# Clustered attention and token mixing on one core: slot lists for the two row halves of the scores, PSUM banks by a plan, and six weight splits moved behind attention

## The chip, the cores and the metric

One core of a Trainium2 chip runs the whole program. The metric is the device time of one execution in microseconds, the median of the runs shown. One profiled execution of the kernel before gives the trace that all durations below come from.

## The reference, cut to what matters

```
# q, k, v: (4, 8, 768, 64), centroids: (8, 16, 64)
q_assign = argmax(normalised q . normalised centroids); k_assign likewise
mask = q_assign[:, :, :, None] == k_assign[:, :, None, :]
scores = where(mask, q k^T / sqrt(64), -1e9)
attn = exp(scores - rowmax); attn /= sum(attn) + 1e-9
x = attn @ v, heads side by side: (4, 768, 512)

theta = x @ w_theta
zr, zi = x * cos(theta), x * sin(theta)
y = w_tok_r @ zr + w_tok_i @ zi          # over the 768 tokens
u = x + y
out = u + maximum(u @ w_ch, 0)
```

The four weights arrive as 64-bit floats, the rest as 32-bit floats.

## The kernel before, in words

**Two stages.** Attention runs first, over 16 pairs of heads (`NPAIR`); each pair has 12 units (`NU`): 2 halves of the query axis (`a`, 384 columns each) times 6 blocks of 128 keys (`i`). So there are 192 units (`NUT`), numbered `u`. The mixing stage follows: for each of the 4 batches 6 token blocks, each with its angle (`theta`, into `tp`) and its share of the token mixing (`mix`, into `y`), then the channel product (`channel`).

**A unit.** The two heads of a pair lie in partitions 0 to 63 (`j` = 0) and 64 to 127 (`j` = 1) of the tiles `hq`, `lq`, `hk`, `lk` (high and low parts of q and k), `mq` and `mk` (one-hot cluster codes, and in row 32 of each half the shift of the row maximum). A score tile `sc` of one unit and one half is four products of 64 rows by 384 columns on PE, and products of the two halves run side by side in PE's two row halves. ACT takes the exponential out of PSUM into `at` (line 437), POOL adds three units of `at` into `acc`, and two units later PE multiplies `at` with v (`av`, line 509). The row maxima come ten units ahead (`LEAD`): a tile `m` is two times two products, and DVE reduces it (line 396).

**A round.** The loop takes two units a round. PE's row halves are filled in twelve steps, here called slots: four with both halves of unit u, four with half 0 of unit u+1 beside the maximum of half 1, then `av` of units u-2 and u-1 and the round's side products, then four with half 1 of u+1 beside the maximum of half 0. Side products are `lg` (cluster logits of a pair three ahead), `lt` and `rt`/`mt` (transposes), and `sm` (row sums). The order on each engine is the order in which the code is written: `in_order` chains the instructions of PE, DVE, ACT, POOL and SP in attention. Tables say at which unit a side job is written (`A_UNITS`, `W_UNITS`, `SUMS`, `NORM`, `ADDS`).

**PSUM.** Of the eight banks the two `m` tiles take four, `av` one, and three banks (`ps`) go round in order for `sc`, `lg`, `rt`, `mt` and `sm`.

**Weights.** A weight is turned from 64 to 32 bits and split in a high and a low part: an absolute value on ACT, four operations on DVE (lines 137 to 146), a copy on ACT (`hi`) and a subtraction on POOL (`lo`). In attention sixteen such chunks are written, one per pair; the last six (the token weights of blocks 3 to 5) are only converted, stored to DRAM (`wd`), loaded again at the start of the mixing stage (`kept`, `late`), and split there with the subtraction on DVE (line 791). `w_ch` is converted there too, through four buffers (`u_tile`). In the mixing stage the scheduler orders the instructions.

Of the kernel before, what the change touches and what calls it, by code (L numbers as in the profile page):

```python
# [19 lines left out]
N_M = 2  # L20
# [21 lines left out]
def kernel(  # L42
# [62 lines left out]
    ncl = cpool.tile([P, 1], F32, name="ncl")  # L105
    nc.vector.tensor_scalar_mul(ncl, mcl, -1.0)
# [43 lines left out]
    def split_w(hi, lo, src, cols, new, eng, most, kept=None):  # L150

        def chunk(sl):
            w = yield from to_f32(src[:, sl], sl.stop - sl.start, new)
            yield
            if kept is not None:
                nc.sync.dma_start(out=kept[:, sl], in_=w)
                return
            nc.scalar.copy(out=hi[:, sl], in_=w)
            eng.tensor_tensor(out=lo[:, sl], in0=w, in1=hi[:, sl].bitcast(F32), op=ALU.subtract)
# [15 lines left out]
    w_d = {(t, x): dram.tile([P, S], F32, name=f"wd{t}{x}") for t in range(EARLY, NT) for x in "ri"}  # L175
# [6 lines left out]
    ps = actx.enter_context(tc.tile_pool(name="ps", bufs=8 - 2 * N_M - N_AV, space=PSUM))  # L182
# [16 lines left out]
    def bank(name):  # L199
        return ps.tile([P, 512], F32, tag="bank", name=name)  # L200
# [47 lines left out]
    def assign(pi):  # L248
# [23 lines left out]
        for t in range(HS // P):  # L272
# [57 lines left out]
        mq = st[pi]["mq"]  # L330
        if pi == 1:

            nc.gpsimd.tensor_scalar(out=mq, in0=cl["q"], scalar1=mcl, scalar2=None, op0=ALU.is_equal)
        else:
# [86 lines left out]
    def score_products(u, j, banks=None):  # L421
# [5 lines left out]
        sc = banks[:, j] if banks else ps.tile([P, 512], F32, tag="bank", name=f"sc{u}_{j}")  # L427
# [88 lines left out]
    def weighted_out(u):  # L516
        pi, a, i = split_u(u)
        s = st[pi]
        if i == NT - 1:

# [14 lines left out]
    def early_weights():  # L535
# [5 lines left out]
        for t in range(EARLY, NT):  # L541
            for x, src in (("r", wrT), ("i", wiT)):
                yield from split_w(
                    None, None, src[t * P:(t + 1) * P], S, raw_pair, nc.gpsimd, CKE, kept=w_d[t, x])
# [107 lines left out]
    A_UNITS = (-9, -4, -2, -1, 2, 2, 3, 6, 7, 7.9)  # L652
# [8 lines left out]
    A_THIRD = (-9, -1, 0, 1, 4, 4, 5, 7, 8, 9)  # L661
    W_EVERY = 12
# [39 lines left out]
    while u <= NUT or todo:  # L702
# [8 lines left out]
        if 0 <= u < NUT:  # L711
            both(score_products, u, exps)
            add_exps(u)
            if ahead < NUT:
                scores_beside_max(u + 1, ahead, 0)
# [6 lines left out]
        if 0 < u <= NUT:  # L722
            weighted(u - 2)
            weighted(u - 1)
            if ahead >= NUT:
                weighted_out(u - 1)
        pieces(u)
        if 0 <= u < NUT:
            if ahead < NUT:
                scores_beside_max(u + 1, ahead, 1)  # L730
            else:

                both(score_products, u + 1, exps, *([m_tile(f"sc{u + 1}")] if u < NUT - 6 else []))
            add_exps(u + 1)
        if 0 < u and ahead < NUT:
            weighted_out(u - 1)
# [270 lines left out]
```

## Time and profile before

| | |
|---|---|
| median of 3 runs (lowest to highest) | 792.06 us (789.42 to 792.98) |
| the profiled execution, its span | 792.87 us, 791.1 us |
| granted TensorE clock over the span | 0.991 |
| PE, DVE, ACT, POOL busy | 774.3, 572.6, 386.5, 488.3 us |
| attention's last exponentials end | about 449.5 us into the span |
| the first token mixing product | 462.23 us into the span |

Busy time of PE is that of matmuls that overlap, so PE reads as busy even where its instructions start later than they could: in attention the starts of successive matmuls have to be read. "Idle before" names the engine whose signal came last. Times inside the span are microseconds from its start.

### The profile page before, as it was taken

The numbers are of one execution on the slowest core, as the hardware profiler recorded it, in microseconds if no ns is written. First come the engines' busy times: TensorE is split into PE (matmuls) and PEld (weight loads), VectorE is DVE, ScalarE is ACT, GpSimd is POOL, SyncE is SP. The second block draws the span as 40 slices with busy tenths as digits, with TensorE's granted clock in tenths as the row PEclk, the third lists the DMA queues.
The fourth block names the chain that finished last, engine by engine and source line by source line (L and its number), as shares of the span: only waits on it lengthen the run. The fifth ranks groups of instructions, "written<-read, shape, count | busy, mean of one in ns | idle before, by whom it ended". The sixth has DMA issues, their size and how long they took to land.

```text
span 791.1 us, 14306 instructions
## 1 busy us (share of the span) xinstructions
PE 774.3 (98%) x5538; PEld 572.9 (72%) x5538; DVE 572.6 (72%) x688; ACT 386.5 (49%) x777; POOL 488.3 (62%) x284
## 2 busy tenths in 40 slices
PE   6999999999999999999999799999999999999998
PEld 4656665666656565656665488899889988899998
DVE  5789999999999999999989659954445433634322
ACT  3366666767676676767556436341334123403310
POOL 3388789999999999888988432561215122332131
PEclk9899999999999999999999999999999999999999
DMA  3132324332433244324343467115011411030001
GB/s 120 61 98 72 93 95 151 93 123 91 151 104 125 81 149 151 119 84 164 112 161 109 101 182 206 24 31 173 15 27 28 160 27 27 14 94 15 1 21 61
DMA packets 81583, 73.43 MB, mean 93 GB/s; under 512 B 59588, under 2 KB 65324, under 8 KB 81132
## 3 DMA queue, kind: packets, MB, share of 16 engines
q1 hardware_dynamic: 81228, 72.10, 30.5%
q8 instruction: 43, 0.70, 0.4%
q10 hardware_dynamic: 288, 0.43, 0.1%
q14 instruction: 24, 0.20, 0.1%
HBM read 57.08 MB, written 15.32 MB: 92 GB/s over the span
## 4 chain that ended last, share of the span: by engine, by line
PE 91%; DVE 5%; DMA 2%; issue 1%; SPq 1%; ACT 1%; DVEq 0%
PE y L876 26%; PE sc L374 24%; PE av L509 15%; PE tp L608 8%; PE cy L899 5%; PE m L374 4%; PE cp L899 3%; PE sm L476 2%; PE lg L263 2%; PE y L899 1%; DVE acc L452 1%; PE lt L275 1%; DVE nm L396 1%; PE mt L404 1%; DVE xl L583 1%
## 5 line engine op out<-in xcount | busy, mean ns | idle before, releaser
L437 ACT ACTIVATE at<-sc 128x384 f32<-128x384 f32 x384 | 173.6, 493 | 96.0 <-PE m L374 50.5
L396 DVE TENSOR_REDUCE nm<-m 128x1 f32<-128x768 f32 x192 | 179.6, 945 | 21.4 <-PE m L374 18.3
L448 POOL TENSOR_TENSOR acc<-at,at 128x768 f32<-128x768 f32 x64 | 129.9, 2030 | 36.0 <-ACT at L437 36.0
L374 PE MATMUL m<-hk,hq 64*128 64x384 f32 x384 | 147.1, 387 | 0.9 <-DVE nm L396 0.8
L509 PE MATMUL av<-at,vt 128*64 128x384 f32 x768 | 145.7, 499 | 1.4 <-ACT at L437 1.2
L830 POOL TENSOR_TENSOR zlc<-ab,zhc 128x512 fp32r<-128x512 f32 x24 | 32.1, 1336 | 173.2 <-ACT zhc L828 173.2
L448 POOL TENSOR_TENSOR acc<-acc,at 128x768 f32<-128x768 f32 x64 | 132.4, 2068 | 10.1 <-ACT at L437 8.0
L374 PE MATMUL m<-mk,mq 64*128 64x384 f32 x384 | 127.7, 336 | 0.8 <-DVE mk L303 0.8
L374 PE MATMUL sc<-hq,hk 64*128 64x384 f32 x384 | 116.6, 388 | 0.5 <-ACT at L437 0.5
L374 PEld LDWEIGHTS sc<-hq,hk 64*128 64x128 f32 x384 | 55.8, 184 | 62.7 <-issue 27.9
L374 PE MATMUL sc<-mq,mk 64*128 64x384 f32 x384 | 97.6, 335 | 0.0
L374 PE MATMUL sc<-hq,lk 64*128 64x384 f32 x384 | 97.3, 334 | 0.0
L374 PE MATMUL sc<-lq,hk 64*128 64x384 f32 x384 | 97.3, 334 | 0.0
L509 PEld LDWEIGHTS av<-at,vt 128*64 128x64 f32 x768 | 46.7, 136 | 60.5 <-issue 53.6
L374 PEld LDWEIGHTS m<-hk,hq 64*128 64x128 f32 x384 | 70.7, 185 | 3.4 <-DVE nm L396 2.8
L374 PEld LDWEIGHTS m<-mk,mq 64*128 64x128 f32 x384 | 71.6, 188 | 1.1 <-ACT hq L356 1.1
L613 DVE TENSOR_SCALAR kk<-tp 128x512 int32<-128x512 f32 x24 | 16.4, 683 | 77.2 <-PE tp L608 77.2
L452 DVE TENSOR_TENSOR acc<-acc,acc 128x768 f32<-128x768 f32 x30 | 70.6, 2354 | 0.0
L581 ACT CAST xh<-xT 128x512 fp32r<-128x512 f32 x23 | 14.3, 622 | 99.7 <-PE tp L608 99.7
L890 POOL TENSOR_TENSOR ul<-xT,uh 128x384 fp32r<-128x384 f32 (+1 forms) x36 | 33.5, 957 | 35.4 <-ACT uh L889 34.9
L374 PEld LDWEIGHTS sc<-lq,hk 64*128 64x128 f32 x384 | 54.9, 186 | 0.0
L374 PEld LDWEIGHTS sc<-mq,mk 64*128 64x128 f32 x384 | 54.7, 184 | 0.0
(160 smaller groups left out, 1710.3 us busy)
## 6 DMA issues: line engine op xcount, KB each, us to landing
rawq<-in_qT_dram SPq DMA_DIRECT2D x16, 384.0 KB
vt<-in_v_dram SPq DMA_DIRECT2D x16, 384.0 KB
rb<-sd SPq DMA_DIRECT2D x32, 192.0 KB
xT_d<-xt SPq DMA_DIRECT2D x16, 384.0 KB
xb<-xT_d SPq DMA_DIRECT2D x96, 64.0 KB
rawk<-in_kT_dram SPq DMA_DIRECT2D x15, 384.0 KB
w<-in_wrT_dram SPq DMA_DIRECT2D x6, 768.0 KB
w<-in_wiT_dram SPq DMA_DIRECT2D x6, 768.0 KB
```

The source lines that it names most:

```text
L374: nc.tensor.matmul(out, lhsT=stat[r, cols], rhs=mov[r, over], start=start, stop=stop)
L396: nc.vector.tensor_reduce(out=s["nm", a][:, j, i // 2:i // 2 + 1], in_=s["m", j][:, :, 0:HS], op=ALU.max, axis=AX.XY, negate=True)
L437: last_exp[0] = nc.scalar.activation(out=s["at", a, i][:, j], in_=s["sc", j], func=AF.Exp, scale=SCALE)
L448: last_acc[0] = nc.gpsimd.tensor_tensor(out=s["acc", a, x], in0=prev, in1=at, op=ALU.add)
L452: nc.vector.tensor_tensor(out=s["acc", a, 0], in0=s["acc", a, 0], in1=s["acc", a, 1], op=ALU.add)
L509: nc.tensor.matmul(s["av"][64 * j:64 * j + 64], lhsT=s["vt"][:, i, j, :], rhs=s["at", a, i][:, j], start=(i == 0), stop=(i == NT - 1))
L608: nc.tensor.matmul(tp, lhsT=xx[:, c, :], rhs=w_th[c][k], start=(n == 0), stop=(n == 3 * NCT - 1))
L613: nc.vector.tensor_scalar_mul(kk, tp, INV_2PI)
L830: nc.gpsimd.tensor_tensor(out=zl, in0=tr, in1=zh.bitcast(F32), op=ALU.subtract)
L876: nc.tensor.matmul(y_at(b, d, c0, c1), lhsT=zz[:, d * P:(d + 1) * P], rhs=ww[:, c0:c1], start=first and lead, stop=last, skip_group_check= ...
L890: nc.gpsimd.tensor_tensor(out=ul[:, d, :], in0=x, in1=uh[:, d, :].bitcast(F32), op=ALU.subtract)
L899: nc.tensor.matmul(cp, lhsT=w_c[d][k][:, e * P:(e + 1) * P], rhs=uu[:, d, :], start=(n == 0), stop=(n == 3 * NCT - 1), skip_group_check=True)
```

## The change

Five things change.

1. **Slot lists.** `two_units` writes the twelve slots of a round with a list for each half. Half 0: the last product left over from the round before (slot 0), a maximum (slots 1 to 4), scores of unit u (5 to 8), scores of unit u+1 (9 to 11, the fourth product carried into the next round's slot 0). Half 1: scores of u (0 to 3), a maximum (4 to 7), scores of u+1 (8 to 11). All of `av` and the side products follow slot 11.
2. **Banks by a plan.** The three banks get a buffer each, and `bank` gives out the one that by a count of slots comes free first: a score tile counts as free five slots after its last product, a side tile eight slots after the round's products.
3. **Assignment codes.** `mk` is made by one ACT operation and `mq` by one DVE operation; before, `mq` took two on ACT and `mk` one on DVE. The comparison `eq` stays in PSUM, and its product with the codes reads PSUM.
4. **Weights.** The six chunks of blocks 3 to 5 are no longer converted in attention. `late` loads them as 64-bit floats through the four `u_tile` buffers, in halves of 384 columns (twelve pieces), converts them and splits them with the subtraction on POOL. The ten that stay are spread at two in three pairs.
5. **Copies of `av`** (`weighted_out`) are written in the next round, behind slot 3.

The diff, cut:

```diff
-    w_d = {(t, x): dram.tile([P, S], F32, name=f"wd{t}{x}") for t in range(EARLY, NT) for x in "ri"}
...
-    ps = actx.enter_context(tc.tile_pool(name="ps", bufs=8 - 2 * N_M - N_AV, space=PSUM))
+    NB = 8 - 2 * N_M - N_AV
+    ps = actx.enter_context(tc.tile_pool(name="ps", bufs=1, space=PSUM))
...
-    def bank(name):
-        return ps.tile([P, 512], F32, tag="bank", name=name)
+    clock = [0.0]
+    free_at = [0.0] * NB
+    SLOTS, AV_SLOTS, EXP_SLOTS = 12, 8, 5
+
+    def bank(name, until=None):
+        x = min(range(NB), key=lambda i: (free_at[i], i))
+        free_at[x] = until if until is not None else clock[0] + AV_SLOTS
+        return ps.tile([P, 512], F32, tag=f"bank{x}", name=name)
...
-            out=eq, in0=ltv, in1=mx.unsqueeze(2).broadcast_to([P, NG, C]), op=ALU.is_equal)
-        yield
-
-        nc.vector.tensor_tensor(out=eq, in0=eq, in1=wb, op=ALU.mult)
+            out=ltv, in0=ltv, in1=mx.unsqueeze(2).broadcast_to([P, NG, C]), op=ALU.is_equal)
+        nc.vector.tensor_tensor(out=eq, in0=ltv, in1=wb, op=ALU.mult)
+        yield
...
-            nc.scalar.activation(out=mq, in_=cl["q"], func=AF.Abs, bias=ncl)
-            yield
-            nc.scalar.activation(out=mq, in_=mq, func=AF.Relu, scale=-1.0, bias=1.0)
+        nc.scalar.activation(out=st[pi]["mk"], in_=cl["k"], func=AF.Abs, scale=kscale, bias=kbias)
         yield
         nc.vector.tensor_scalar(
-            out=st[pi]["mk"], in0=cl["k"], scalar1=mcl, scalar2=mbi, op0=ALU.not_equal, op1=ALU.mult)
+            out=st[pi]["mq"], in0=cl["q"], scalar1=mcl, scalar2=-1.0, op0=ALU.is_equal, op1=ALU.mult)
...
-    def scores_beside_max(u, v, j):
-
-        interleave(score_products(u, j), max_products(v, 1 - j))
-        exps(u, j)
-        max_of(v, 1 - j)
+    carry = []
...
+    def two_units(u, v):
+        rows = {(0, 0): carry[0]} if carry else {}
+        first = [(exps, u - 1, 0), (add_exps, u - 1)] if carry else []
+        carry.clear()
+        t0 = clock[0]
+
+        def scores(u, j, start, until):
+            for slot, x in enumerate(score_products(u, j, until=t0 + until + EXP_SLOTS), start):
+                if slot < SLOTS:
+                    rows[j, slot] = x
+                else:
+                    carry.append(x)
...
+        begin = {
+            0: (scores, u, 1, 0, 4), 1: (maxima, 0, 1), 4: (maxima, 1, 4), 5: (scores, u, 0, 5, 9),
+            8: (scores, u + 1, 1, 8, 12), 9: (scores, u + 1, 0, 9, SLOTS + AV_SLOTS + 1)}
+        end = {
+            0: first, 3: [(exps, u, 1), (weighted_out, u - 3)], 4: [(max_of, v, 0)], 7: [(max_of, v, 1)],
+            8: [(exps, u, 0), (add_exps, u)], 11: [(exps, u + 1, 1)]}
...
-    A_UNITS = (-9, -4, -2, -1, 2, 2, 3, 6, 7, 7.9)
+    A_UNITS = (-9, -4, -2.5, -1, 2, 2, 3, 7, 7.9)
...
-        stages(W_FIRST if x == 0 else [W_EVERY * (x - 1) + k for k in W_UNITS], gen)
+        stages(W_FIRST if x == 0 else [NU * (3 * (x - 1) // 2) + k for k in W_UNITS], gen)
...
-            for w, x in ((w_r, "r"), (w_i, "i")):
-                hi, lo = w[t]
-                kept = u_tile("kept").rearrange("p c s -> p (c s)").bitcast(F32)[:, 0:S]
-                nc.sync.dma_start(out=kept, in_=w_d[t, x])
-                nc.scalar.copy(out=hi, in_=kept)
-                nc.vector.tensor_tensor(out=lo, in0=kept, in1=f(hi), op=ALU.subtract)
+            for w, src in ((w_r, wrT), (w_i, wiT)):
+                for gen in split_w(*w[t], src[t * P:(t + 1) * P], S, wt_pair, nc.gpsimd, CK):
+                    run(gen)
```

**PE, round of unit 92, where `mt` and `lg` are written.** Names read: `sc93_0` is unit 93, half 0; `m102_1` a maximum; `av`, `mt` and `lg` as above. Before:

```order
L374 MATMUL sc93_0_3153<-mq_1_147,mk_1_148 128x384
L374 MATMUL m102_1_3155<-mk_2_157,mq_2_156 128x384
L509 MATMUL av90_3168<-at90_3084,vt7_2781 64x384 x2
L509 MATMUL av90_3168<-at91_3097,vt7_2781 64x384 x2
L404 MATMUL mt80_3177<-identf_64,nm96_2977 6x128
L263 MATMUL lg10_3183<-rawq10_3024,cb_194 32x384
L263 MATMUL lg10_3183<-rawk10_3026,cb_194 32x384
...
L374 MATMUL sc93_1_3193<-hq_1_143,hk_1_145 128x384
L374 MATMUL m102_0_3194<-hk_2_154,hq_2_152 128x384
L374 MATMUL sc93_1_3193<-lq_1_144,hk_1_145 128x384
```

With the change:

```order
L378 MATMUL sc93_0_3142<-hq_1_145,lk_1_148 128x384
L378 MATMUL sc93_1_3137<-mq_1_149,mk_1_150 128x384
L552 MATMUL av90_3152<-at90_3056,vt7_2753 64x384 x2
L552 MATMUL av90_3152<-at91_3082,vt7_2753 64x384 x2
L408 MATMUL mt80_3161<-identf_64,nm96_2938 6x128
L273 MATMUL lg10_3167<-rawq10_2997,cb_196 32x384
L273 MATMUL lg10_3167<-rawk10_2999,cb_196 32x384
...
L378 MATMUL sc93_0_3142<-mq_1_149,mk_1_150 128x384
L378 MATMUL sc94_1_3180<-hq_1_145,hk_1_147 128x384
L378 MATMUL m104_0_3184<-hk_2_156,hq_2_154 128x384
L378 MATMUL sc94_1_3180<-lq_1_146,hk_1_147 128x384
```

The fourth product of `sc93_0` now stands behind `av`, `mt` and `lg`. In this round `mt` and `lg` take the two banks that the plan has free, so `sc94_1`, the next row, is given the bank of `sc93_0` itself. That is so in 13 rounds (u = 8, 20, ... 152). In 32 other rounds, after a single side tile, the score tile that begins in slot 5 has the bank of the tile that ended in slot 0; in the plain rounds the closest reuse is slot 3 to slot 9.

**ACT at the same place.** `mr` and `lgs` copy `mt` and `lg` out of PSUM; `wi` is a weight's high part. Before:

```order
L437 ACTIVATE at93_3152<-sc93_0_3153 128x384
L158 CAST wi1_hi_115<-w32_2837 128x768
L415 CAST mr80_3179<-mt80_3177 6x128
L267 COPY lgs10_3188<-lg10_3183 128x384
L437 ACTIVATE at93_3152<-sc93_1_3193 128x384
```

With the change:

```order
L441 ACTIVATE at93_3136<-sc93_1_3137 128x384
L161 CAST wi0_hi_121<-w32_2822 128x768
L419 CAST mr80_3163<-mt80_3161 6x128
L277 COPY lgs10_3172<-lg10_3167 128x384
L441 ACTIVATE at93_3136<-sc93_0_3142 128x384
L441 ACTIVATE at94_3179<-sc94_1_3180 128x384
```

The exponential of `sc93_0` has moved behind the two copies.

**POOL, first batch of the mixing stage.** `zlc` and `zls` are the low parts of the rotated block (batch, block), `wr4_lo` that of a token weight. Before:

```order
L830 TENSOR_TENSOR zlc0_3_6242<-ab0_3_6231,zhc0_3_6241 128x512
L830 TENSOR_TENSOR zls0_3_6248<-r0_3_6212,zhs0_3_6247 128x512
L159 TENSOR_TENSOR wch0_lo_6039<-wtmp_6358,wch0_hi_6038 128x512
L830 TENSOR_TENSOR zlc0_4_6341<-ab0_4_6330,zhc0_4_6340 128x512
L830 TENSOR_TENSOR zls0_4_6347<-r0_4_6311,zhs0_4_6346 128x512
```

With the change:

```order
L867 TENSOR_TENSOR zlc0_3_6204<-ab0_3_6193,zhc0_3_6203 128x512
L162 TENSOR_TENSOR wr3_lo_5961<-wtmp_6080,wr3_hi_5960 128x384
...
L162 TENSOR_TENSOR wi3_lo_5963<-wtmp_6107,wi3_hi_5962 128x384
L867 TENSOR_TENSOR zls0_3_6210<-r0_3_6174,zhs0_3_6209 128x512
L162 TENSOR_TENSOR wr4_lo_5965<-wtmp_6213,wr4_hi_5964 128x384
L867 TENSOR_TENSOR zlc0_4_6331<-ab0_4_6320,zhc0_4_6330 128x512
L867 TENSOR_TENSOR zls0_4_6337<-r0_4_6301,zhs0_4_6336 128x512
L162 TENSOR_TENSOR wr4_lo_5965<-wtmp_6222,wr4_hi_5964 128x384
```

Twelve subtractions of 384 columns now stand among POOL's rotations, and with each of them a buffer comes free for the next load. PE's order in the mixing stage is the same as before.

More of the change, by code (lines that the diff above doesn't have):

```diff
@@ L419, in shift_out, with score_products @@
                 in_=f(mr[j * NH:(j + 1) * NH]))
-    def score_products(u, j, banks=None):
+    def score_products(u, j, banks=None, until=None):
         pi, a, i = split_u(u)
@@ L426, in score_products @@
             s["at", a, i] = p3.tile([P, 2, HS], F32, tag="at", name=f"at{u}", bufs=NAT)
-        sc = banks[:, j] if banks else ps.tile([P, 512], F32, tag="bank", name=f"sc{u}_{j}")
+        sc = banks[:, j] if banks else bank(f"sc{u}_{j}", until)
         sc = s["sc", j] = sc[:, 0:HS]
@@ L726 @@
                 weighted_out(u - 1)
+        clock[0] = (u / 2 + 1) * (SLOTS + AV_SLOTS)
         pieces(u)
[L728 to L733, printed above, removed]
+        if 0 <= u < NUT and ahead >= NUT:
+            both(score_products, u + 1, exps, *([m_tile(f"sc{u + 1}")] if u < NUT - 6 else []))
             add_exps(u + 1)
-        if 0 < u and ahead < NUT:
-            weighted_out(u - 1)
         pieces(u + 1)
```

58 lines of the change are left out of this document (38 added, 20 removed).

## The prediction

> **What bounds the kernel now.** I read the page first, then the stretches, then the chain of waits in order of time, then PE's and ACT's instructions in order of time.
>
> ```profile
> PE 774.3 (98%) x5538; PEld 572.9 (72%) x5538; DVE 572.6 (72%) x688; ACT 386.5 (49%) x777; POOL 488.3 (62%) x284
> L374 PE MATMUL m<-hk,hq 64*128 64x384 f32 x384 | 147.1, 387 | 0.9 <-DVE nm L396 0.8
> 160.00:200.00 40.00, 40.00 (x333) 24.63 (x332) 38.12 (x39) 26.46 (x56) 38.94 (x20) 1.00 0.31 98
> 148.31 1.03 PE sc L374 x10
> 174.26 1.03 PE sc L374 x10
> ```
>
> The first row gives PE 98%. The third is a stretch of attention (busy PE, PEld, DVE, ACT, POOL, then clock): PE is full, DVE has 38.12 of 40 us and POOL 38.94, so three engines are close to the bound. The second says which of them ends last: in the whole run the first product of a maximum waited 0.8 us for DVE. So PE sets the pace, and DVE and POOL just keep up. The chain goes through the same place of successive pairs at 148.31 and 174.26: a pair costs 25.95 us, six rounds. What PE wastes must be read from the starts of its rows, since its busy time counts overlapping matmuls:
>
> ```profile
> 177.20 0.44 PE L374 MATMUL sc<-hq,hk 64*128 64x384 f32 x1
> 177.48 0.33 PE L374 MATMUL sc<-lq,hk 64*128 64x384 f32 x1
> 178.00 0.34 PE L374 MATMUL sc<-hq,hk 64*128 64x384 f32 x2
> 178.52 0.34 PE L374 MATMUL sc<-mq,mk 64*128 64x384 f32 x2
> 178.74 0.44 PE L374 MATMUL sc<-hq,hk 64*128 64x384 f32 x1
> 179.02 0.33 PE L374 MATMUL sc<-lq,hk 64*128 64x384 f32 x1
> 181.08 0.27 PE L404 MATMUL mt<-identf,nm 128*6 128x128 f32 x1
> 182.06 0.44 PE L374 MATMUL sc<-hq,hk 64*128 64x384 f32 x1
> 199.24 0.44 PE L374 MATMUL sc<-hq,hk 64*128 64x384 f32 x1
> ```
>
> ```profile
> 178.20 0.49 ACT L437 ACTIVATE at<-sc 128x384 f32<-128x384 f32 x1 [0.96 <-PE m L374]
> 179.69 1.25 ACT L437 ACTIVATE at<-sc 128x384 f32<-128x384 f32 x3
> 182.20 0.48 ACT L267 COPY lgs<-lg 128x384 f32<-128x384 f32 x1 [0.42 <-PE lg L263]
> 199.38 0.58 ACT L482 ACTIVATE se<-sm,eps 128x384 f32<-128x384 f32 x1 [1.71 <-PE sm L476]
> ```
>
> From 178.00 to 178.52 three slots take 0.52, so a slot is 0.173 us. From 178.52 to 178.74 there is 0.22, and the next step is 0.28 where it should be 0.173: a wait of 0.047 and a restart of 0.107, 0.154 in all. The releaser is ACT: the exponential that began at 178.20 ends at 178.69, 0.05 ahead of the row at 178.74. It empties the bank that this score tile takes, the third back in the ring.
>
> From the same rows come the prices of a hand-over. The group that began at 177.20 has its last product at 177.48 + 2 x 0.173 = 177.83, which ends 0.33 later; the exponential starts 0.04 after, takes 0.49, and PE starts 0.05 after that. Three exponentials in 1.25 us stand 0.38 apart, so on ACT one operation begins 0.11 before the last one's end.
>
> **The change part by part.**
>
> *Slot lists and banks, plain rounds.* The 0.154 goes if no other reuse is late. In the new list the closest plain one is slot 3 to slot 9. Counted from slot 0, whose successor is 0.28 later as at 177.20, slot 3 starts at 0.28 + 2 x 0.173 = 0.63, and its bank is free at 0.63 + 0.33 + 0.04 + 0.49 + 0.05 = 1.54; slot 9 comes at 0.28 + 8 x 0.173 = 1.66. So it holds, by 0.12 us. Rounds with both lists run from u = 0 to 180: 91 x 0.154 = 14.0 us gained. The ends are 14.0 and 10, if the margin fails in a quarter.
>
> *The 13 rounds with* `mt` *and* `lg`. There `sc94_1` takes the bank of `sc93_0`, one row ahead of it, and PE must wait for a whole hand-over with all else queued behind it. In the trace the first score after `lg` starts at 182.06. There the carried product now runs: it ends 0.44 later and could be read at 182.54. But ACT has `lgs` first, until 182.68; the exponential follows at 182.57, ends at 183.06, PE goes on at 183.11. That is 1.05 us late, 13 x 1.05 = 13.7 us. The lower end is the hand-over without `lgs` in the way, 0.44 + 0.04 + 0.49 + 0.05 = 1.02 (13.3); the upper, with no overlap on ACT, 1.2 (15.6). It takes back nearly all of the gain.
>
> *The 32 places where slot 5 reuses slot 0.* Bank free at the earliest at 1.02, as just added; slot 5 comes at 0.28 + 4 x 0.173 = 0.97. So a wait of 0.05 and a restart of 0.107: 0.16, after `mt` alone, 16 times: 2.5 us. After `sm`, ACT has `se` first, from 199.38 to 199.96: the exponential runs from 199.85 to 200.34, PE goes on at 200.39 instead of 199.24 + 0.97 = 200.21: 0.18 + 0.107 = 0.29, 16 times: 4.6 us. Together 7.1. The ends are 0 (the 0.05 is no more than the trace's starts can be read to) and 14 (casts that stand ahead of the carried exponential delay it by as much again). I take 7.1, since both parts come from rows of the same rounds.
>
> *DVE's side work in attention.* Six chunks leave, and `eq` times the codes reads PSUM. Worth nothing: PE waited 0.8 us for it. If it slowed, its cover is the idle share of the third row, 1.9 of 40 us, and what leaves widens that. `mk` and `mq` exchange engines with one ACT operation less: nothing, as ACT has 26.46 of 40. The copies of `av` now stand behind slot 3, and the next `av` follows slot 11, eight slots or 1.4 us later: nothing.
>
> *The mixing stage.* Six weights are now converted at its start.
>
> ```profile
> 480.00:500.00 20.00, 20.00 (x109) 17.21 (x108) 19.93 (x26) 11.55 (x20) 8.31 (x5) 1.00 0.55 161
> 470.00:495.00 25.00, 7.62 (x6) 1.00 0.74 221
> L137 DVE TENSOR_SCALAR wtmp<-wtmp 128x512 f32<-128x512 f32 x4 | 2.8, 693 | 0.0
> L140 DVE TENSOR_SCALAR wtmp<-wtmp 128x512 int32<-128x512 int32 x4 | 2.1, 536 | 0.0
> L143 DVE SCALAR_TENSOR_TENSOR wtmp<-wtmp 128x512 int32<-128x512 int32 x4 | 3.8, 958 | 0.0
> L146 DVE SCALAR_TENSOR_TENSOR wtmp<-wtmp 128x512 int32<-128x512 int32 x4 | 2.7, 680 | 0.0
> L159 POOL TENSOR_TENSOR wch_lo<-wtmp,wch_hi 128x512 fp32r<-128x512 f32 x4 | 5.8, 1455 | 13.7 <-ACT wch_hi L158 13.7
> 481.79 0.61 ACT L828 CAST zhc<-ab 128x512 fp32r<-128x512 f32 x1
> 483.28 0.43 SPq L130 DMA_DIRECT2D wtmp<-in_w_ch_dram  x1
> 487.94 0.67 ACT L135 ACTIVATE wtmp<-wtmp 128x512 f32<-128x512 f32 x1 [0.80 <-DMA wtmp<-in_w_ch_dram]
> 504.37 0.50 PE L876 MATMUL y<-wr_hi,zhc 128*128 128x512 f32 x2
> 515.52 0.50 PE L876 MATMUL y<-wr_hi,zhc 128*128 128x512 f32 x2
> ```
>
> DVE is full there (19.93 of 20 us). The four `wtmp` rows sum to 2.87 us for 512 columns, 2.15 for a piece of 384, so 12 pieces are 25.8 us; the second row is the line that leaves DVE (line 791), 7.62 us. What counts is whether blocks 4 and 5 are ready when PE reaches them, at 504.37 and 515.52. Block 3's pieces are loaded before and split behind the cast at 481.79; with a high-part copy of about half a microsecond and a POOL subtraction of 1.09 each (three quarters of 1.46) the four buffers come free from 484 to 487. A load takes 4.66 (issued at 483.28, read at 487.94), so block 4's lie there from 488.5 to 492; 8.6 of DVE and the split end at about 500, 4 ahead of 504.37. Block 5's buffers come free from 492 to 500, the last load lands at 504.7, then 2.15, up to 5 of rotation work on DVE in between and 1.6 of split: 508.5 to 513.5, 2 to 7 ahead of 515.52. So the lower end is 0. The upper end: if every DVE conversion beside a POOL subtraction waits it out, 8 x 1.09 = 8.7 more in these two blocks, 7 us late. I take 1.5, near the means.
>
> By the Trainium skill ("SBUF — State Buffer", section "Terms", on the port pair that VectorE and GpSimd share) the first to take the pair holds it for its whole instruction and the other blocks; by that page the term would be nearer 7 than 0. The 958 ns of line 143 against 680 of line 146 for the same shape agrees that something like it happens, without saying how often.
>
> *The end of attention.*
>
> ```profile
> 436.87 0.32 SPq L156 DMA_DIRECT2D wd5i<-w  x1
> 437.47 1.07 PE L608 MATMUL tp<-wth_hi,xl 128*128 128x512 f32 x4
> 439.37 0.23 DVE L494 RECIPROCAL sq<-sq 128x12 f32<-128x12 f32 x1 [2.53 <-DMA sq<-sd]
> 441.01 1.16 PE L608 MATMUL tp<-wth_hi,xh 128*128 128x512 f32 x4 [1.40 <-DVE r L614]
> ```
>
> The store of the last converted weight held SP until 436.87; the load of `sq` stood behind it, DVE's reciprocal waited for that until 439.37, and the angle's reduction behind it. Without the store DVE can start when `tp` ends, at 438.54: 0.9 earlier, and PE's 1.40 of waiting at 441.01 shortens by that. The ends are 0 and 1.4. I take 0.9.
>
> *Sum*, against the profiled execution's 792.87 us (the median of the runs is 792.06): -14.0 + 13.7 + 7.1 + 1.5 - 0.9 = +7.4, so **800 us**.
>
> **The rivals.** A measurement of this kernel can tell about 0.5% (4 us) from no change.
>
> *Faster: the gaps around* `av` *are waits too.*
>
> ```profile
> 429.88 0.34 PE L374 MATMUL sc<-mq,mk 64*128 64x384 f32 x2
> 430.15 1.51 PE L509 MATMUL av<-at,vt 128*64 128x384 f32 x8
> ```
>
> PE loses 0.10 into each `av` (0.27 instead of 0.173) and 0.11 out of it (177.20 to 177.48). Were these waits for ACT or DVE, the lists would remove them: 91 x 0.204 = 18.6 us more, 782 us. Against it: the rows above are of the last units, where no maxima run, and show the same 0.27. It decides from 0.08 a round, where the sum changes sign.
>
> *No change:* slot 5 never waits and the conversions stay hidden, so gain and bank wait cancel: 792.87 - 14.0 + 13.7 - 0.9 = 791.7. For it speaks that slot 5's wait is 0.05, the size of what I can read.
>
> *Slower still: the weights bind.* Block 5 comes 7 us late, 800.3 + 5.5 = 806; for it speaks the full DVE at 480 to 500, against it the spare I worked out.
>
> *The clock.* 13 waits of a microsecond might lower the granted clock.
>
> ```profile
> 438.00:441.00 3.00, 1.61 (x12) 0.95 (x11) 1.56 (x4) 1.16 (x3) 0.55 (x1) 1.00 0.29 92
> 452.00:454.00 2.00, 1.12 (x8) 0.46 (x12) 2.00 (x4) 0.67 (x2) 1.01 (x1) 0.50 0.86 195
> ```
>
> With 1.40 us of waiting in one piece the clock stayed at 1.00; only after several such gaps did it fall to 0.50. If each wait cost about 7 us at half speed, as around 452, 13 x 3.5 = 45 us would come on top: 845. The Trainium skill ("TensorE: Matmul & The Clock Gate", section "A second HAM failure mode: psum-queue depth-cycling") tells of such a kernel, whose short idle gaps between groups make the gate go up and down. The row at 438 speaks against it here.
>
> **How the numbers follow.** The forecast (797 to 804) has 0.44; no change at 791.7 0.28; weights at 806 0.15; `av` gaps at 782 0.10; clock at 845 0.03. The range takes in the two middle rivals and the bounds: below, all low ends but the gain, 792.87 - 14.0 + 13.3 - 1.4 = 790.8, and 3 for the spread of runs (789.42 to 792.98), 788; above, 800.3 + 6.9 for slot 5 and 5.5 for the weights, 813. Faster by over 0.5%: 0.10. Within: 0.30, the no-change case and the forecast's lower edge. Slower: 0.60.
>
> **What would show it.** Right: a pair with `lg` takes about 26.5 us (25.95 - 6 x 0.154 + 1.05 + 0.16 + 0.29), one without 25.5; once per pair PE is idle for about a microsecond behind `lg`, released by an exponential; the plain rounds are 0.15 shorter and have no late step at mid-round; DVE shows idle time in attention. Wrong: no idle piece behind `lg`; a plain round as long as before; the first products of blocks 4 and 5 late, released by `wr` or `wi`; a clock below 1 in attention.

## The result, and the profile after

The changed kernel takes 824.07 us (median of 4 runs, 823.38 to 824.74) against 792.52 us for the kernel before: ratio 1.0406, 95% interval 1.0377 to 1.0436. It is 31.5 us slower where 7 were forecast (800 us). The profiled executions have spans of 821.7 and 791.1 us, 30.6 us apart. Of all executions one alone was slow, 2532 us among the four of e2_lg_apart below (the others took 854 to 859), and it is left out there.

The page's first row, and from the chain of work that ended last the starts of two `av` groups at the same place of successive pairs:

```profile
PE 778.7 (95%) x5538; PEld 575.3 (70%) x5538; DVE 545.8 (66%) x713; ACT 391.4 (48%) x776; POOL 481.0 (59%) x295
128.66 1.44 PE av L552 x8
155.37 1.44 PE av L552 x8
```

PE has the same 5538 instructions and nearly the same busy time, but 95% instead of 98% of the span: it waits more. A pair took 25.95 us and takes 26.71.

`av` closes each round, so the starts of its rows divide the span at the same 97 places in every kernel. The table is worked out from them. Lead-in is the start of the first `av`, body runs from there to the 82nd (the rounds with both lists), the tail to the last, mixing to the end of the span.

| | lead-in | body | tail | mixing | span |
|---|---|---|---|---|---|
| before | 36.57 | 350.70 | 61.91 | 341.9 | 791.1 |
| after | 39.86 | 360.11 | 62.40 | 359.3 | 821.7 |
| lost | 3.3 | 9.4 | 0.5 | 17.4 | 30.6 |

So more than half of the loss is in the stage for which the forecast had 1.5 us.

**Attention.** Windows of the stretch shown of before and of the place where mixing stalls (busy PE, PEld, DVE, ACT, POOL, then clock), and PE's and ACT's rows in order of time:

```profile
160.00:200.00 40.00, 38.50 (x320) 23.73 (x318) 38.39 (x37) 24.94 (x52) 36.12 (x19) 1.00 0.28 87
520.00:540.00 20.00, 16.82 (x90) 13.77 (x88) 19.86 (x33) 12.13 (x24) 10.19 (x8) 1.00 0.42 129
540.00:580.00 40.00, 30.22 (x143) 27.30 (x144) 24.33 (x40) 11.81 (x23) 18.21 (x16) 0.79 0.31 92
```

```profile
155.30 1.51 PE L552 MATMUL av<-at,vt 128*64 128x384 f32 x8
159.07 1.51 PE L552 MATMUL av<-at,vt 128*64 128x384 f32 x8
161.50 0.44 PE L378 MATMUL sc<-mq,mk 64*128 64x384 f32 x1
162.56 0.44 PE L378 MATMUL sc<-hq,hk 64*128 64x384 f32 x1 [0.62 <-ACT at L441]
175.49 0.34 PE L378 MATMUL m<-hk,hq 64*128 64x384 f32 x1
175.70 0.44 PE L378 MATMUL sc<-hq,hk 64*128 64x384 f32 x1
180.18 0.34 PE L378 MATMUL m<-hk,hq 64*128 64x384 f32 x1
180.53 0.44 PE L378 MATMUL sc<-hq,hk 64*128 64x384 f32 x1
```

```profile
161.64 0.48 ACT L277 COPY lgs<-lg 128x384 f32<-128x384 f32 x1 [0.56 <-PE lg L273]
162.01 0.50 ACT L441 ACTIVATE at<-sc 128x384 f32<-128x384 f32 x1
```

A plain round is 3.77 us (155.30 to 159.07), 0.10 shorter than before. Behind `lg` the carried product starts at 161.50 and the next score at 162.56, 1.06 later: `lgs` stands ahead of the exponential that frees the bank, and the releaser is that exponential. Behind `mt` slot 5 starts 0.21 after slot 4 (175.49 to 175.70), behind `sm` 0.35 (180.18 to 180.53). These are the three waits of the prediction, at its sizes (a slot being 0.173). VectorE, busy for 342 of the 360 us from 40 to 400 before, is busy for 301 of them now.

**Mixing.** PE at the first product of the stage, in block 5 and ahead of the channel; SP's loads of the channel weight; ACT's last high part of it; two VectorE rows of one line. Then the counterparts of before:

```profile
474.43 0.51 PE L913 MATMUL y<-wr_hi,zhc 128*128 128x512 f32 x2
529.96 0.62 PE L913 MATMUL y<-wi_hi,zhs 128*128 128x512 f32 x2 [1.03 <-ACT wi_hi L161]
531.41 0.62 PE L913 MATMUL y<-wi_lo,zhs 128*128 128x512 f32 x2 [0.84 <-POOL wi_lo L162]
549.42 1.01 PE L936 MATMUL cp<-uh,wch_hi 128*128 128x384 f32 x2 [10.74 <-ACT uh L926]
522.33 2.96 SPq L136 DMA_DIRECT2D wtmp<-in_w_ch_dram  x2
531.74 0.57 SPq L136 DMA_DIRECT2D wtmp<-in_w_ch_dram  x1
547.74 0.62 ACT L161 CAST wch_hi<-wtmp 128x512 fp32r<-128x512 f32 x1 [2.53 <-DVE wtmp L152]
539.74 1.75 DVE L149 SCALAR_TENSOR_TENSOR wtmp<-wtmp 128x512 int32<-128x512 int32 x1
544.49 0.68 DVE L149 SCALAR_TENSOR_TENSOR wtmp<-wtmp 128x512 int32<-128x512 int32 x1
```

```profile
506.77 0.62 ACT L158 CAST wch_hi<-wtmp 128x512 fp32r<-128x512 f32 x1
523.93 0.51 PE L899 MATMUL cp<-uh,wch_hi 128*128 128x384 f32 x2
```

The first product of the stage is 12.2 us later than before (462.23). Block 5 loses 1.9 us more. Then PE stands for 10.74 us. Before, the last part of the channel weight was ready at 507.4, 16.5 ahead of the channel's first product; now it is ready at 548.4. Its loads go out only from 522 to 532, when the twelve pieces give back the four buffers, and VectorE (19.86 of 20 us) converts it ahead of the addition that makes `uh`. Behind this pause the granted clock is 0.50 until 555 (0.79 over the 40 us of the window): from 549.42 to the next batch the channel takes 5 us longer. (A few of the channel's products also stand in another order than before; elsewhere in the stage PE's order is the same.)

VectorE from the stage's first product to the last high part of the channel weight, before and after (busy time is the third):

```profile
462.23:507.39 45.16, 45.16 (x248) 38.97 (x247) 36.81 (x50) 19.84 (x33) 14.32 (x10) 1.00 0.50 140
474.43:548.36 73.93, 62.39 (x338) 53.09 (x336) 65.76 (x103) 31.22 (x58) 34.49 (x26) 0.95 0.46 125
```

The stretch is 28.8 us longer and VectorE's busy time in it 29.0; its idle time, 8 us, is the same.

### The profile page after: what moved, and what is told of

Read it like the earlier page. It is cut to its first block, busy times and chain, and to the rows that moved or that the text cites. A ratio compares the mean times of both kernels' runs of the same rounds, so it can differ in the third digit from the quotient of the medians.

```text
span 821.7 us, 14377 instructions
## 1 busy us (share of the span) xinstructions
PE 778.7 (95%) x5538; PEld 575.3 (70%) x5538; DVE 545.8 (66%) x713; ACT 391.4 (48%) x776; POOL 481.0 (59%) x295
## 4 chain that ended last, share of the span: by engine, by line
PE 81%; DVE 9%; DMA 3%; ACT 3%; issue 2%; SPq 1%; POOL 0%; DVEq 0%; ACTq 0%; POOLq 0%
PE sc L378 19%; PE y L913 19%; PE av L552 16%; PE m L378 8%; PE tp L649 6%; PE cy L936 5%; PE cp L936 3%; PE lg L273 2%; PE sm L519 1%; DVE wtmp L149 1%; PE y L936 1%; PE lt L285 1%; ACT at L441 1%; DVE nm L400 1%; DVE wtmp L152 1%
## 5 line engine op out<-in xcount | busy, mean ns | idle before, releaser
L441 ACT ACTIVATE at<-sc 128x384 f32<-128x384 f32 x384 | 186.6, 491 | 102.1 <-PE sc L378 81.9
L378 PE MATMUL sc<-hq,hk 64*128 64x384 f32 x384 | 127.2, 382 | 9.8 <-ACT at L441 8.8
L378 PE MATMUL sc<-mq,mk 64*128 64x384 f32 x384 | 135.1, 359 | 0.0
L378 PE MATMUL m<-hk,hq 64*128 64x384 f32 x384 | 119.2, 346 | 1.5 <-DVE eq L292 0.9
L378 PE MATMUL sc<-lq,hk 64*128 64x384 f32 x384 | 112.5, 340 | 0.0
L378 PE MATMUL sc<-hq,lk 64*128 64x384 f32 x384 | 110.1, 334 | 0.0
L378 PEld LDWEIGHTS sc<-mq,mk 64*128 64x128 f32 x384 | 69.3, 184 | 47.4 <-issue 46.8
L378 PEld LDWEIGHTS sc<-hq,hk 64*128 64x128 f32 x384 | 68.4, 183 | 30.5 <-ACT at L441 21.8
L654 DVE TENSOR_SCALAR kk<-tp 128x512 int32<-128x512 f32 x24 | 16.5, 687 | 78.6 <-PE tp L649 78.6
L378 PEld LDWEIGHTS sc<-hq,lk 64*128 64x128 f32 x384 | 68.0, 185 | 0.0
L622 ACT CAST xh<-xT 128x512 fp32r<-128x512 f32 x23 | 14.3, 620 | 99.0 <-PE tp L649 99.0
L456 DVE TENSOR_TENSOR acc<-acc,acc 128x768 f32<-128x768 f32 x30 | 56.3, 1878 | 2.9 <-POOL acc L452 2.9
```

The costliest lines, as they stand in the source:

```text
L378: nc.tensor.matmul(out, lhsT=stat[r, cols], rhs=mov[r, over], start=start, stop=stop)
L441: last_exp[0] = nc.scalar.activation(out=s["at", a, i][:, j], in_=s["sc", j], func=AF.Exp, scale=SCALE)
L456: nc.vector.tensor_tensor(out=s["acc", a, 0], in0=s["acc", a, 0], in1=s["acc", a, 1], op=ALU.add)
L654: nc.vector.tensor_scalar_mul(kk, tp, INV_2PI)
```

## The experiments

Durations below are of one profiled execution each; "body" and the other stretches are those of the table above.

| run | median us | ratio to before (95%) | lead-in | body | mixing |
|---|---|---|---|---|---|
| e1_hold | 817.4 | 1.031 (1.028 to 1.034) | 41.5 | 353.6 | 358.8 |
| e2_lg_apart | 857.1 | 1.082 (1.080 to 1.085) | 43.3 | 388.3 | 357.2 |
| e3_old_weights | 808.5 | 1.020 (1.019 to 1.022) | 43.2 | 361.1 | 339.4 |
| e4_no_conv | 813.0 | 1.026 (1.025 to 1.028) | 43.3 | 360.1 | 346.8 |
| e5_hold_oldw | 801.0 | 1.015 (1.010 to 1.019) | 41.0 | 354.0 | 342.1 |
| e6_lists_only | 800.8 | 1.014 (1.011 to 1.017) | 39.3 | 354.5 | 340.9 |
| e7_codes_only | 804.7 | 1.019 (1.016 to 1.022) | 41.1 | 360.3 | 341.0 |
| e8_weights_only | 807.2 | 1.022 (1.019 to 1.026) | 35.2 | 350.7 | 356.2 |
| e9_lists_hold8 | 818.8 | 1.034 (1.030 to 1.038) | 38.5 | 374.1 | 341.0 |
| e10_wch_first | 827.6 | 1.044 (1.040 to 1.047) | 41.7 | 361.0 | 359.8 |
| e11_lists_mended | 795.4 | 1.004 (1.002 to 1.006) | 36.9 | 354.1 | 341.8 |
| e12_banks_acc | 811.0 | 1.026 (1.022 to 1.030) | 39.5 | 347.3 | 358.8 |

None beats the kernel before. The fifth part of the change, the later copies of `av`, goes with the slot lists in every run and was not tried alone.

**The bank waits (e1_hold).**

```diff
-        free_at[x] = until if until is not None else clock[0] + AV_SLOTS
+        free_at[x] = until if until is not None else clock[0] + 3
-        lg = bank(f"lg{pi}")[:, 0:HS]
+        lg = bank(f"lg{pi}", clock[0] + 5)[:, 0:HS]
```

> Only the plan's holding time of side tiles is changed: a bank of mt, rt or sm counts as free three slots after the round's products, one of lg five, where it was eight. Then the score tile behind mt and lg takes the bank of mt instead of that of the carried scores, and slot 5 takes the bank of the side tile instead of that of slot 0. Theory A (PE waits for late banks): the round with lg falls from 6.30 us to about 5.4, the one with mt from 4.22 to 4.07, the one with sm from 4.82 to 4.54, a pair from 26.69 to 25.4, the whole from 824 to about 806. Rival B (the order of the copies on ACT makes those rounds long, whichever bank is taken): the pair stays at 26.7 and the time at 822 to 825.

The rounds came out as theory A has them: with `mt` 4.09, with `sm` 4.58, with `lg` 5.24 where nothing else was late. But only 6.5 us of the body came back, and the time, 817.4, lies between the two theories. The groups of PE between 45 and 400 us (busy, mean, then idle before and its releaser), first of the changed kernel, then two of this run:

```profile
L378 PE MATMUL sc<-hq,hk 64*128 64x384 f32 x320 | 107.4, 380 | 8.5 <-ACT at L441 8.4
```

```profile
L285 PE MATMUL lt<-identf,lgs 128*128 128x128 f32 x39 | 7.1, 291 | 8.9 <-DVE nm L400 8.9
271.87 0.55 PE L285 MATMUL lt<-identf,lgs 128*128 128x128 f32 x3 [3.03 <-DVE nm L400]
266.13 2.24 DVE L343 TENSOR_SCALAR mq<-clq,mcl 128x768 fp32r<-128x768 f32 x1
268.29 2.57 DVE L456 TENSOR_TENSOR acc<-acc,acc 128x768 f32<-128x768 f32 x1
270.92 1.75 DVE L400 TENSOR_REDUCE nm<-m 128x1 f32<-128x768 f32 x2
```

The 8.4 us of waiting for banks are gone, and 8.9 us at `lt` have come in their place, in the same rounds. `lt` takes a buffer of the maxima, which VectorE reduces only after `mq` and an addition of `acc`, 4.8 us together. Both ran beside additions of POOL here; the shortest of their kind in this run took 0.61 and 0.94 us. In the changed kernel this wait lay under the one ahead of it.

**lg in a round of its own (e2_lg_apart).** The second entry of `A_UNITS` is -6 instead of -4.

> Only lg is moved, one round ahead, so that mt and lg never stand in one round; everything else as in the changed kernel. Theory A (two side tiles in one round take both free banks): the 13 waits of 1.06 us behind lg go, each for one slot-5 wait behind lg (0.35) and one behind mt (0.2); a pair falls from 26.69 to about 26.2, the whole to about 818. Rival B (the copy lgs ahead of the carried exponential is what makes PE wait): the long wait moves along with lg to its new round, time 823 to 825.

Neither: `lg` now came ahead of its data. Rows of PE's groups, and one wait behind `lg` with ACT's row at that time:

```profile
L273 PE MATMUL lg<-rawk,cb 128*32 128x384 f32 x48 | 10.2, 498 | 8.2 <-DMA rawk<-in_kT_dram 8.2
228.86 0.44 PE L378 MATMUL sc<-hq,hk 64*128 64x384 f32 x1 [0.81 <-ACT at L441]
227.39 1.03 ACT L341 ACTIVATE mk<-clk,kbias,kscale 128x768 fp32r<-128x768 f32 x1
```

The round with `lg` took 7.2 to 8.9 us, PE waiting for the load. The run still shows two things. Without `lg`, whose own products take 0.8 us, the round with `mt` and `lt` took 4.86 against 6.30, and the first products of its two halves start together (231.94 and 231.95) where they were 1.06 apart: that wait left it. And in the new round slot 5 waited 0.81 where 0.35 was expected, since `mk` (1.03 us) stood on ACT between `lgs` and the exponentials: how long a late bank costs is set by what ACT has first, so rival B was right about that part.

**The weights (e3_old_weights, e8_weights_only).** The one undoes the fourth part of the change, the other makes it alone.

```diff
-            for w, src in ((w_r, wrT), (w_i, wiT)):
-                for gen in split_w(*w[t], src[t * P:(t + 1) * P], S, wt_pair, nc.gpsimd, CK):
-                    run(gen)
+            for w, x in ((w_r, "r"), (w_i, "i")):
...
+                nc.sync.dma_start(out=kept, in_=w_d[t, x])
...
+                nc.vector.tensor_tensor(out=lo, in0=kept, in1=f(hi), op=ALU.subtract)
```

> The six weight chunks go back to where they were before the change: converted in attention at one per pair, stored, loaded and split at the start of the mixing stage. Slot lists, banks, codes and lead-in stay as changed. Theory C (the mixing stage loses 18.4 us because the twelve pieces and the channel weight behind them come late): block 5 and the channel products start as soon as the products ahead are done, as in the kernel before; the store holds the end of attention up by 0.9 again; 824 - 18.4 + 0.9 = 806.5. Rival D (the lower clock and the later start are what stretches the mixing stage): under 5 us come back, 819 or more. If VectorE, fuller again in attention, cannot keep up with the shorter rounds, pairs get longer than 26.69 by up to 0.5 each and the time lands near 812.

> The kernel before with the late conversion of the six token weights alone. Theory C (the mixing stage is made late by the twelve pieces wherever attention ends): 17 to 20 us come on top in the mixing stage, 0.9 go at the end of attention, pairs stay at 25.95: 809 to 812. Rival F (it is late only because the rest of the change shifted the loads and the work at the end of attention): under 10 on top, 795 to 802.

Theory C in e3; e8's 807.2 lies between C and F, nearer C. Without the twelve pieces mixing takes 339.4 us, with them alone 356.2, 14.3 more than before; PE's wait ahead of the channel is there as well. One window of e3, one group of e8:

```profile
540.00:580.00 40.00, 40.00 (x221) 36.35 (x220) 15.42 (x28) 10.12 (x18) 13.77 (x13) 1.00 0.34 98
L888 PE MATMUL cp<-uh,wch_hi 128*128 128x384 f32 x8 | 3.3, 477 | 10.4 <-ACT uh L878 10.3
```

In all runs but e4 (below) the stage falls in two groups: 339 to 342 us with the old weights, 356 to 360 with the new. The expected 17 to 20 was 14.3 without the other parts; the remaining 3 of the 17.4 go with them and were not separated. VectorE with six chunks more in attention did not lengthen the body by more than 1 us in e3.

**What in mixing (e4_no_conv, e10_wch_first).** In e4 the four VectorE operations of the twelve pieces are left out. In e10 the loop over `w_ch` stands ahead of the loop over the token weights.

> The changed kernel without the four VectorE operations that turn the twelve late pieces of the token weights to 32 bits (their values are then those of the upper halves, so the output is not the reference's); loads, the absolute value, the copy to the high part and the subtraction stay, and so does the whole conversion of the channel weight. Theory C1 (VectorE's 25.8 us of conversions delay the channel weight): the channel of batch 0 starts about 17 us earlier, with no wait of PE ahead of it, 806 to 808. Rival C2 (the loads, which wait for four buffers and for SP, set the time): the loads of the channel weight are still issued late, PE waits over 6 us ahead of the channel, 815 to 822.

> The changed kernel with the channel weight converted ahead of the twelve pieces, in the first two batches of late work. Theory K (the last pair's normalisation on VectorE queues behind the first four pieces' conversions; its store frees the memory of the first high parts 17 us later than before; the four buffers stand still until then, and the channel weight comes last of all): the channel weight is ready before it is wanted, the 10.7 us of waiting ahead of the channel and its half clock go, the token pieces of block 4 or 5 may come up to 8 us late instead: 806 to 816. Rival L (VectorE's work alone sets the end, in whatever order): block 5's weights come as late as the channel weight did, 820 to 828.

```profile
541.44 0.62 PE L938 MATMUL cp<-uh,wch_hi 128*128 128x384 f32 x2 [2.11 <-ACT uh L928]
```

In e4 mixing took 346.8 us: VectorE's operations on the pieces are 12.6 of the 17.4, and 4.8 are left, with the loads and splits of the pieces still going through the same four buffers. The wait ahead of the channel (row above) is 2.11 instead of 10.74. The time, 813.0, lies between C1 and C2; it was over the 806 to 808 of C1 also because the lead-in was 3.4 longer.

In e10 (ACT's row of the channel weight's high parts, and PE's first wait):

```profile
497.67 2.18 ACT L161 CAST wch_hi<-wtmp 128x512 fp32r<-128x512 f32 x4 [0.94 <-issue]
515.92 2.50 PE L913 MATMUL y<-wr_hi,zhc 128*128 128x512 f32 x6 [5.11 <-ACT wr_hi L161]
```

The channel weight was ready in time and the wait ahead of the channel is gone. Block 3 then waited 5.1 us and the blocks behind it 6.7 in all, and mixing took 359.8: rival L. All high parts stood until 497.67, 4.9 us after the last store of attention was issued at 492.82; that part of theory K the trace shows. But whichever weight came first, the last high part was ready at nearly the same time (552.2 in e10, 548.4 in the changed kernel, whose stage began 2.5 earlier), so the order is not the cause.

**The parts of attention alone (e7_codes_only, e6_lists_only, e9_lists_hold8).** e7 is the kernel before with the third part of the change, `A_UNITS` with it. e6 and e9 are the slot lists and the bank plan on the weights and codes of before, with short and with long holding times.

> The kernel before with the new assignment codes alone (mk on ACT, mq on VectorE, the comparison kept in PSUM, the two new constants). Theory E (the lead-in's 3.3 us come from these, as VectorE's chain ahead of the first maxima is longer and PE falls to half clock in the waits): first av at 38.5 to 42 us, 796 to 798, pairs as before. Rival: the lead-in got longer through the slot lists or the weights; the time stays at 792 to 794.

> The slot lists and the bank plan with the shorter holding times, on the weights and the assignment codes of the kernel before. Theory A (the lists gain where no bank and no VectorE result is late): first av at 36.6 us as in the kernel before, the plain rounds 3.78 against 3.87, mt 4.09 against 4.19, sm 4.58 against 4.69, lg and lt together 9.04 against 9.32; 0.69 us a pair, 783 to 786 in all. Rival B (VectorE, 96% busy in attention before, cannot give the maxima in time for lt in the shorter rounds): lt waits 0.7 us or more a pair, 790 to 796.

> The slot lists and the bank plan as changed (side tiles hold for eight slots), on the weights and codes of the kernel before, so with lt behind av again. Theory H (behind lg there were two waits on one path: the scores' for their bank and, behind it, lt's for VectorE; the first covered the second): against the run of the lists with short holding the bank wait comes back alone, 0.9 us in 13 rounds and 0.15 to 0.3 in 32: the round with lg 5.6 us (4.71 there), the pair 27.0 against 25.9 less what VectorE then no longer makes lt's successor wait (0.44), 26.5 to 27.0; 809 to 815. Rival: the bank wait costs nothing once lt is back behind av; the pair stays near 26, 800.

The codes alone cost the lead-in 4.5 us and, what no theory had, the body 9.6; so the time, 804.7, is over both theories. A group of e7:

```profile
L281 PE MATMUL lt<-identf,lgs 128*128 128x128 f32 x39 | 7.1, 291 | 9.5 <-DVE nm L395 9.4
```

`lt` was moved by the third entry of `A_UNITS` (-2 to -2.5) from behind `av` to ahead of it, and there it waits for the maxima. (No run moves `lt` alone; e7 has the codes with it.) The rounds of `lg` and `lt` together, in a steady pair:

| | bank wait behind `lg` | `lt` ahead of `av` | both rounds, us |
|---|---|---|---|
| before (other lists) | no | no | 9.32 |
| e7 (other lists) | no | yes | 10.07 |
| e6 | no | no | 9.59 |
| e1 | no | yes | 9.04 and the wait at `lt`, 0.7 a pair |
| e9 | yes | no | 10.66 |
| after | yes | yes | 10.10 |

With the lists, the bank wait alone adds 1.07 (e9 to e6), the one at `lt` alone 0.7 (e1), and both together 1.06 (10.10 against e1's 9.04): the first covers the second, as theory H has it. The rival is out. But e9 itself was slower than H, 818.8 with a pair of 27.7 (its rounds in a steady pair: 5.78, 4.88, 4.16, 4.21, 4.80, 3.89): behind `av`, `lt`'s successor waited as in e6, and nothing was covered there.

e6, 800.8, was slower than both theories had it. Its steady pair is 25.91, no better than before, and its first pairs take 26.2 to 28.3: the rounds with `mt` and `sm` gained 0.10 each, but `lt`, back behind `av`, holds the second maximum's buffer until its comparison is done:

```profile
271.83 0.41 PE L383 MATMUL m<-hk,hq 64*128 64x384 f32 x1 [0.27 <-DVE eq L288]
```

**Both edits (e5_hold_oldw).** e1 and e3 together.

> Both earlier edits together: side tiles hold their banks for three and five slots, and the six weight chunks are back in attention. Additive theory: the bank edit gave 6.7 us and the weights 15.6 against the changed kernel's 824.1, together 802. Rival: in the bank edit's run lt waited 8.9 us for VectorE's maxima in place of the 8.4 that the scores had waited for their bank; with six more chunks on VectorE that wait grows, by up to one chunk's 4 us in each of six pairs, and the time lands at 805 to 815.

They add: 801.0 against 802. The wait at `lt` was 10.6 us with six more chunks on VectorE, 8.9 without.

**VectorE behind the banks (e11_lists_mended, e12_banks_acc).** Both have short holding times, a plan whose choice goes round, `lt` ahead of `av`, and one addition of `acc` three units later; e11 on the codes and weights of before, e12 on those of the change.

```diff
-    clock = [0.0]
-    free_at = [0.0] * NB
+    clock = [-1e6]
+    free_at = [-1e6] * NB
+    used = [0] * NB
-        x = min(range(NB), key=lambda i: (free_at[i], i))
+        x = min(range(NB), key=lambda i: (free_at[i], used[i]))
+        used[x] = max(used) + 1
-ADDS = (8, 13)
+ADDS = (11, 13)
```

> The slot lists on the weights and codes of the kernel before, with four edits: short holding times; a bank plan whose choice among equally free banks goes round, with its clock far back at the start (in the lead-in the plan's clock stood still and gave every side tile the same bank); lt ahead of av; and VectorE's addition of acc of the first half moved from unit 8 to unit 11, behind lt's reductions. Theory M: first av back at 36 to 38 us (39.3 in the run of the lists with short holding), lg and lt rounds 9.1 us together (9.59 there), the pair 25.4 (25.9 there, 25.95 before): 785 to 790 where the kernel before has 789 to 793. Rival: lt still waits for VectorE's maxima, 0.5 us or more a pair: 793 to 798.

> The changed kernel (codes, weights and lt as changed) with the shorter holding times, the bank choice that goes round with its clock far back at the start, and the addition of acc of the first half moved from unit 8 to unit 11. Theory N (with the banks free, what is left in the round of lg is lt's wait for VectorE, which stands 2.6 us in that addition; with a third of the chunks gone from attention VectorE has room for it elsewhere): lt's wait falls from 8.9 us to under 2, a pair to about 25.3, first to 82nd av 345 us or less (360 in the changed kernel, 351 before), lead-in 38 to 41, the mixing stage still 17 longer: 804 to 808. Rival (the addition makes the maxima behind it late instead, as it did with all chunks in attention): the pair stays over 25.7, 812 to 816.

A row of e12's groups between 45 and 400 us each for `lt` and the maxima, then a wait of e11 and VectorE's row at that time:

```profile
L287 PE MATMUL lt<-identf,lgs 128*128 128x128 f32 x39 | 7.1, 291 | 0.4 <-DVE nm L402 0.4
L380 PE MATMUL m<-hk,hq 64*128 64x384 f32 x332 | 99.5, 336 | 3.1 <-DVE nm L402 3.1
```

```profile
297.23 0.44 PE L385 MATMUL m<-hk,hq 64*128 64x384 f32 x1 [0.52 <-DVE nm L407]
293.73 1.99 DVE L294 TENSOR_TENSOR eq<-eq,wc 128x384 bf16<-128x384 bf16 x1
```

In e12 the wait at `lt` fell from 8.9 us to 0.4. An undisturbed pair takes 25.3 us, and the body 347.3, 3.4 less than before; some pairs still lose up to 1.6 to late maxima, so it is less than theory N's 345. The time, 811, lies between the two theories; the 17 us in mixing stay. In e11, with all chunks on VectorE, the waits went from `lt` to the maxima behind it, and the body is 354.1: the rival. The lead-in is back to 36.9, as expected.

## Why the prediction was wrong, step by step

The sum was +7.4 us, the spans show +30.6. Of the 23.2 between them 15.9 are the mixing stage, 3.3 the lead-in and 4.0 the rest of attention.

- **Mixing, the step that failed.** "What counts is whether blocks 4 and 5 are ready": it is not. The working followed the pieces to block 5, where it was not far off: that block was 1.9 us late, the term was 1.5. It left out what stands behind them, the channel weight, which needs the same four buffers and 11.5 us of VectorE (four pieces of 2.87). Block 5's last load was worked out to land at 504.7; the channel weight's loads had to follow that, and 16.5 us of slack ahead of the channel's first product were there to be read in the trace of before. The sum was there to be made: by the prediction's own rows 25.8 us of VectorE come to the stage and 7.6 leave it, 18.2 more on an engine that the row at 480 shows full, against those 16.5. The runs show that in its place: without the pieces' conversions 12.6 of the 17.4 us are gone (e4), and the order of the weights changes nothing (e10). The rival "the weights bind" had the right stage and engine, and the wrong victim: 806 instead of 824. The rule of the Trainium skill on the port pair ("SBUF — State Buffer", section "Terms") points the right way: line 149 took 1.75 us at 539.74, beside a subtraction on POOL, and 0.68 at 544.49. VectorE's operations on the twelve pieces took 30.5 us instead of the 25.8 worked out; at the shortest of each kind they would be 20.2, and 9.5 of the 10.2 above that fall in operations that ran beside one of POOL. No run here took POOL's subtractions away, so what of this stands on PE's path is open.
- **Plain rounds.** The gain is 0.10 a round, not 0.154: the first to the last row of slots takes 2.07 us (156.74 to 158.81) where the prediction's steps make 2.01. By whole pairs it is 0.69 (25.95 to the 25.26 of e1's undisturbed pair), not 0.92; 91 rounds make 9 to 10.5, not 14.
- **`mt` and `lg`.** This step was right: the wait is 1.06 for 1.05 expected, and since all twelve products of the other half follow it, the round pays it in full (6.30 against e1's 5.24). 13 rounds make 13.8.
- **Slot 5.** 0.13 behind `mt` and 0.24 behind `sm` by the rounds of e1 (4.22 to 4.09, 4.82 to 4.58), against 0.16 and 0.29: 5.9 us for 7.1. With the two terms above that makes 9.2 at the larger gain, where the body shows 9.4.
- **`lt`, not priced.** The earlier place in `A_UNITS` was shown in the diff and has no term. With the codes, on the kernel before, it costs 9.6 us (e7), and in the changed kernel it lies under the bank wait. So the body's +9.4 comes near the predicted 6.8 for more than one reason: mending the banks alone brings back 6.5 and uncovers `lt`'s wait.
- **The lead-in, not priced.** DVE's side work was put at nothing by attention's steady rounds alone. In the lead-in PE waits for VectorE's chain, and the codes lengthen it; the bank plan's clock stands still there, and its two `ot` tiles get one bank. PE's rows of before and of after:

```profile
6.88 0.45 PE L231 MATMUL cps<-identf,cnn 128*128 128x128 f32 x1 [1.57 <-DVE cnn L226]
```

```profile
7.74 0.30 PE L241 MATMUL cps<-identf,cnn 128*128 128x128 f32 x1 [2.44 <-DVE cnn L236]
14.40 0.51 PE L308 MATMUL ot<-identb,clq 128*128 128x128 bf16 x6 [1.18 <-DVE clq L301]
15.79 0.50 PE L308 MATMUL ot<-identb,clq 128*128 128x128 bf16 x6 [0.89 <-ACT mq L311]
```

  The second row of the first maximum's products comes 1.3 us later (16.09, then 17.40); with the codes alone it is at 17.43 (e7), with the lists and the plan alone at 16.65 (e6). With the codes of before and the plan mended (e11) the lead-in is 36.9. The rest of the 3.3 goes with the clock, below; no run separates it.
- **The end of attention.** 0.9 expected (its rows give 0.83); from the 94th to the 95th `av` 10.74 became 9.86, as forecast. The tail's other rounds lost 1.4, for which there was no term.
- **The clock.** That rival is out for attention: 1.00 in the stretch with two of the long waits, and over all of 40 to 400. The rule of the Trainium skill on short gaps ("TensorE: Matmul & The Clock Gate", section "A second HAM failure mode: psum-queue depth-cycling") doesn't show here with one microsecond a pair. Behind the lead-in the clock fell at the end of attention, as it did before (0.57 from 466 to 470), and behind the 10.74 us.

## What to carry to other kernels

When work is moved to a stage, follow the resources that it takes (buffers, the engine's queue) to the last user in that stage, not only to the first product that needs the moved work; the slack of that last user is a row of the trace of before. When a wait is taken away, look on the same engine for the next wait in the same round: two that overlap cost no more than one, and mending one of them gives back less than its price. A plan that counts time must count it everywhere that it is used, the lead-in too.

## What was not expected of the hardware

The same lead-in code took 39.9 us in the changed kernel and 43.2 in e3 and e4. Windows of the two (clock third from the end of the row), first the changed kernel, then e3:

```profile
8.00:14.00 6.00, 4.07 (x36) 2.49 (x35) 2.69 (x7) 0.48 (x1) 0.00 (x0) 0.72 0.40 131
26.00:34.00 8.00, 7.34 (x43) 4.77 (x43) 4.66 (x6) 1.76 (x3) 0.00 (x0) 0.59 0.30 88
```

```profile
18.00:22.00 4.00, 4.00 (x27) 2.13 (x27) 1.82 (x2) 0.48 (x1) 4.00 (x3) 0.57 0.36 101
28.00:40.00 12.00, 11.35 (x66) 8.01 (x66) 6.67 (x9) 3.46 (x7) 0.00 (x0) 0.57 0.18 62
```

PE ran at half clock at other times and for longer, 12 us around 34 instead of 8 around 30. So a few microseconds of any difference between these kernels can be the lead-in's clock (e8, which leaves the lead-in as before, had 35.2 for 36.6), which is why the stretches are compared apart. And the same multiplication of the codes (128x384, 16 bits) took 1.99 us in e11 at 293.73, beside an addition of POOL that ended 0.22 ahead of it, where the one of before that ran undisturbed, at 12.14, took 0.36. In the changed kernel, where this product reads the comparison from PSUM, all sixteen took 0.56.
